# A fused RWKV-7 and GELU kernel: each piece of weights in four transfers of 2560-byte rows in place of one of 10240-byte rows

## The chip, the cores and the metric

The kernel runs on one core of a Trainium2 chip. The metric is the time of one execution on the device, in microseconds (us), given as the median of several runs. Engines are named as in the profile: PE is TensorE's matrix multiply and PEld its weight load, DVE is VectorE, ACT is ScalarE, POOL is GpSimd, and SP is SyncE, which here does nothing but issue DMA transfers. A "block" below means 256 instructions of one engine.

## The reference

Two parts follow each other. The first is a linear attention with a state per head (4 batches, 8 heads, 768 steps, head size 40), which runs through time:

```python
for t in range(S):
    y[:, :, t] = np.einsum('bhd,bhde->bhe', rt, state)
    Sa = np.einsum('bhde,bhe->bhd', state, at)
    state_decay = state * wt[:, :, None, :] - np.einsum('bhd,bhe->bhde', Sa, bt)
    state = state_decay + np.einsum('bhd,bhe->bhde', vt, kt)
```

Its output, as 3072 rows of 320, goes through a two-layer network with a hidden size of 2048:

```python
h = x @ w_in
g = h * (1.0 / (1.0 + np.exp(-1.702 * h)))
return (g @ w_out).astype(np.float32)
```

The inputs of the attention are float32. The two weight matrices, w_in (320 x 2048) and w_out (2048 x 320), come as float64 and are made into float32 on the chip.

## The kernel before

**Units and chunks.** Time is cut into 12 chunks of 64 steps. A unit is one chunk of two of the four batches, so there are 24 units, and units 2c and 2c+1 make up chunk c. For each unit the kernel forms decays, scores, a triangular inverse in five levels (`inverse`, with a transpose on DVE or a copy on ACT between levels), solves for the rows, reads the output and hands the state on to unit i+2 (`solve`). Unit i's output tile x goes out to DRAM and comes back transposed into `xT_all` (L983 and L987), because the network wants the channels on the partitions. When both units of a chunk are back, `mlp(c)` multiplies by w_in (`ps_up`), applies GELU on ACT and multiplies by w_out (`ps_down`).

**Weights.** The float64 weights come in eight pieces, four of w_in and four of w_out. A piece is 128 rows of 1280 float64 numbers: 10240 bytes a row, 1,310,720 bytes in all. `weight(n, rank, src)` loads piece n (L498) into one of four raw places: two in the tile `extra` ("a" and "b"), two in parts of `w_sb` that are not yet in use ("w4" and "w6"), and one piece in `xT_all` ("x"), so pieces 5, 6 and 7 wait until a raw place is free again. Five instructions then make float32 of a piece: one on ACT (L478, about 1.4 us), three on DVE (L482, L486, L490, about 0.8 us each where nothing holds them up), one on POOL (L494, about 3 us). The eight pieces are in flight or being converted between 13 us and 115 us of the span.

**Other loads.** Each unit loads ak, b and rv (`load`, L533, two transfers of 40 rows each, rows of 4096, 2048 and 4096 bytes), RV (128 rows of 1280 bytes), time (128 rows of 2560 bytes) and logw (L520, 1280 bytes); from unit 4 on also wc (L520, 2112 bytes).

**Order of the work.** Nothing is scheduled by hand and nothing while the kernel runs. Every piece of work is a task with a rank, the engines that can do it with a cost in ns, what it reads and writes, and a size if it is a transfer. `Plan.order` simulates the engines with these costs, and the order in which it starts the tasks is the order of the instructions on each engine. Of the tasks that are able to start, the one with the lowest rank is taken. `Plan.refined` then draws 300 random changes of ranks from a generator with a fixed seed (`TRIES, SEED`), keeps one if the simulated end comes earlier, and so changes the order of the work whose start the first simulation put before 140 us. The simulation also counts that PE's instructions come in blocks of 256 by DMA, and that this takes longer while transfers run; a transfer of over 1,000,000 bytes (`LARGE`) weighs more in this than others do:

```python
BESIDE, LARGE, BESIDE_LARGE = 0.35, 1e6, 0.63
...
took = self.FETCH + sum(w * max(0.0, min(y, at + took) - max(x, at)) for x, y, w in running[-10:])
...
wire = max(wire, end + self.LATENCY)
running.append((wire, wire + self.SPREAD * t.size / self.RATE, self.BESIDE_LARGE if t.size > self.LARGE else self.BESIDE))
```

`wire` is the simulated time at which the transfers issued so far are through; `running` holds them with their weights, and only the last ten are looked at.

**SP's queue.** SP issues all transfers, one after the other, in planned order. An issue takes 0.33 to 0.41 us in the trace (L498). The trace also shows that eight completion semaphores are taken in turn, and that an issue does not happen before the transfer that last took its semaphore, the eighth before it, has landed. The data of the transfers run on one queue, named q1 in the profile, and PE's instruction blocks come on another, q8, both over the same 16 DMA engines.

The function that the diff touches, with its calls:

Of the kernel before, what the change touches and what calls it, by code (L numbers as in the profile page):

```python
# [279 lines left out]
def rwkv7_gelu_quick(ctx: ExitStack, tc: tile.TileContext, time_d, v_d, w_d, wc_d, ak_d, b_d, rv_d, w_in, w_out, out):  # L280
    nc = tc.nc
# [5 lines left out]
    PIECE = w_in.shape[2]  # L287
# [6 lines left out]
    EARLY = 4  # L294
    BY_PE = 4
    PLAIN = 4
    ROUNDS, WINDOW, SHARE = 4, 5000.0, 1.0
    TRIES, SEED = 300, 1
    RANKS = [14, 16, 20, 24, 35, 37, 39, 41]
    HALF = [slice(0, 64), slice(64, 128)]  # L300
    BITS = (0, 1)
# [8 lines left out]
    plan = Plan(dict(logw=3, wc=3, G=1, wch=3, wz=2, time=2, ak=2, b=2, rv=2, FT=3, GT=1, kh=2, bh=2, zr=2, rz=2,  # L310
                     A=1, B=1, RV=2, E0=2, W0=2, P21=2, PT=2, W=2, E=2, ES=2, EX=2, T=2, Tc=1, QT=1, zraw=2, zT=1, M=2, x=1, xT=3, g=4, ob=1), 4)
# [17 lines left out]
    def mm(o, lhsT, rhs, start):  # L329
        nc.tensor.matmul(o, lhsT, rhs, start=start, stop=True, skip_group_check=True)  # L330
# [5 lines left out]
    def pe(*sets):  # L336

        return {"PE": sum(n * 2 * max(58.0, cols / 1.2 + 3) for n, cols in sets), "instr": sum(16 * n for n, _ in sets)}

    def dve(n):  # L340
        return {"DVE": 170.0 + 1.03 * n}

    def act(n):
        return {"ACT": 210.0 + 0.76 * n}
# [7 lines left out]
    def of(e):  # L352
        return nc.gpsimd if e == "POOL" else nc.vector
# [77 lines left out]
    def preset(engine, *places):  # L431
        for t in places:
            copy(engine)(t, one32.unsqueeze(1).to_broadcast([128, 8, 32]))
# [28 lines left out]
    def weight(n, rank, src):  # L462
        at = raws[n]
        def raw():
            if at == "x":
                return xT_all[:, 1:].rearrange("p s n -> p (s n)").bitcast(INT64)
            tile, k = spots[at]
            return tile[:, k * PIECE:(k + 2) * PIECE].bitcast(INT64)

        scale = lambda: w_sb[:, n * PIECE:(n + 1) * PIECE].bitcast(INT32)  # L470

        before = [("weight", m) for m in range(n) if raws[m] == at]
        there = [("weight", m) for m in range(n) if raws[m] in (f"w{n}", f"w{n - 1}")]
        word = lambda dt, w: raw().bitcast(dt).rearrange("p (n two) -> p n two", two=2)[:, :, w]

        def rebased(t):

            nc.scalar.activation(scale().bitcast(FP32), word(FP32, 1), ACT.Prelu, scale=2.0 ** -112, alpha=2.0 ** 32)  # L478

        def bounded(t):  # L480

            nc.vector.tensor_scalar(scale().bitcast(FP32), scale().bitcast(FP32), least, most, ALU.max, ALU.min)  # L482

        def shifted(t):

            nc.vector.tensor_single_scalar(scale(), scale(), 3, op=ALU.logical_shift_left)  # L486

        def rounded(t):

            nc.vector.tensor_single_scalar(word(INT32, 1), word(UINT32, 0), 2.0 ** -29, op=ALU.mult)  # L490

        def joined(t):

            nc.gpsimd.tensor_tensor(out=scale(), in0=scale(), in1=word(INT32, 1), op=ALU.add)  # L494

        one, add = 170.0 + 0.52 * PIECE, 200.0 + 2.1 * PIECE
        T = lambda *names: [(name, n) for name in names]
        plan.add(rank, {"SP": 350.0}, lambda t: nc.sync.dma_start(raw(), src), reads=before, writes=T("wt"), size=128 * PIECE * 8)  # L498
        plan.add(rank, act(PIECE), rebased, reads=T("wt") + there, writes=T("rebased"))
        plan.add(rank, {"DVE": one, "sbuf": True}, bounded, reads=T("rebased"), writes=T("bounded"))  # L500
        plan.add(rank, {"DVE": one, "sbuf": True}, shifted, reads=T("bounded"), writes=T("parts"))
        plan.add(rank, {"DVE": one, "sbuf": True}, rounded, reads=T("rebased"), writes=T("parts"))
        plan.add(rank, {"POOL": add}, joined, reads=T("parts"), writes=T("weight"))

    def weights():
        for n in range(len(raws)):
            weight(n, RANKS[n], w_in[n] if n < NQ else w_out[n - NQ])
# [184 lines left out]
    def inverse(i):  # L692
# [10 lines left out]
        PT = at(PT_t, i).rearrange("p (j t) -> p j t", t=96)  # L703
        if i < PLAIN:
            plan.add(R - 3, {"ACT": 400.0}, lambda t: preset(t.engine, PT[:, :, 64:]), room=T("PT"), writes=T("preset"))
        elif i < PLAIN + 2:
            plan.add(R - 3, {"ACT": 800.0, "DVE": 900.0}, lambda t: preset(t.engine, at(E0_t, i), at(W0_t, i)[:, :, 32:]), room=T("PT"),
                     writes=T("preset"))

        def score_N(t):  # L710

            ps = psum(t, "ps_N")
            for f, u in product(BITS, BITS):
                for e, b in QUARTERS:
                    o, j = (2 * f + u) * 64, slot(b, u, f)
                    mm(ps[HALF[b], e, o:o + 64], ahT()[HALF[e], j], b_of(i)[HALF[e], j], o == 0)
        plan.add(R, pe((4, 64)), score_N, reads=T("ahT", "bhT") + (T("preset") if i < PLAIN + 2 else []), uses=T("ak", "b"), room=T("E0", "P21"), pair=("N", i))
        for n in BITS if i >= PLAIN else ():
            plan.add(R, dve(256), lambda t, n=n: nc.vector.copy_predicated(  # L719
# [4 lines left out]
                 writes=T("P21"), pair=("N", i))  # L724
        if i >= PLAIN:
            plan.add(R, {"DVE": 430.0, "POOL": 750.0, "sbuf": True}, lambda t: of(t.engine).tensor_sub(  # L726
                at(W0_t, i)[:, :, :32], two32.unsqueeze(1).to_broadcast([128, 8, 32]), at(E0_t, i)), reads=T("E0"), writes=T("W0"))

        def turned(rank, source, reads, n, dst, writes):

            plan.add(rank, dve(256), lambda t: nc.vector.transpose(ES(n), source(t)), writes=[key("ES", n, 6)], **reads)  # L731

            def spread(t):
                if t.engine == "ACT":
                    for h in BITS:
                        nc.scalar.activation(dst[:, :, h], ES(n), ACT.Copy, scale=quads[:, h, :1])  # L736
                else:
                    of(t.engine).tensor_mul(dst, ES(n).unsqueeze(2).to_broadcast([128, 8, 2, 32]),
                                            quads.unsqueeze(1).to_broadcast([128, 8, 2, 32]))
            plan.add(rank, {"POOL": 1390.0, "DVE": 700.0, "ACT": 910.0, "sbuf": True}, spread, reads=[key("ES", n, 6)], writes=writes)  # L740

        if i >= PLAIN:
            turned(R, lambda t: at(E0_t, i), dict(reads=T("E0")), 0, EX(0), [key("EX", 0, 5)])
# [411 lines left out]
```

## Time and profile before

| what | value |
|---|---|
| median of 3 runs | 713.35 us (712.49 to 715.39) |
| the profiled execution, its own time | 715.64 us |
| its span, first to last instruction | 713.9 us |
| PE busy | 673.0 us, 94% of the span |
| DVE, ACT, POOL busy | 59%, 49%, 29% |
| packets of 10240 bytes (weights), from the trace's record of packets | 1024, median 388 ns each |
| packets of 2560 bytes (time) | 6144, median 102 ns, three quarters below 127 ns |
| packets of 16384 bytes on q8 (instruction blocks) | 159, median 1048 ns |

The page's rows of digits cut the span into 40 slices of 17.8 us and give in tenths how busy each engine is in each slice, what part of full speed the clock granted to PE, and how busy the DMA engines are. The windows view gives the same as numbers for stretches that one chooses. A timeline lists an engine's instructions in order; in square brackets stands the idle time before an instruction and what ended it. "issue" there means that nothing that the profile shows ended it: no semaphore came, the instruction simply wasn't there earlier. The chain of waits follows the work that ended last back from the end.

### The profile page before, as it was taken

The page shows a single profiled execution, that of the slowest core. Times are in us where ns is not written, and L with a number is a line of the kernel's source. Part 1 is how long each engine was busy: PE and PEld are TensorE (multiplying, and loading weights), DVE is VectorE, ACT ScalarE, POOL GpSimd, SP SyncE. Part 2 cuts the span into 40 slices and gives each one's busy share as a digit, 9 for nine tenths or more (in the row PEclk, how much of TensorE's full clock was granted, in tenths as well). Part 3 has the DMA queues.
Part 4 walks back from the last instruction along what each step waited for, and adds up shares of the span by engine and source line. Part 5 has one row for each costly group of instructions (what it writes and reads, how often), then busy time and mean ns, then how long its engine had stood idle before and what let it go on. Part 6 is the DMA issues. An engine that isn't in the chain of part 4 may idle for free.

```text
span 713.9 us, 43522 instructions
## 1 busy us (share of the span) xinstructions
PE 673.0 (94%) x20256; PEld 562.4 (79%) x20256; DVE 423.8 (59%) x747; ACT 347.7 (49%) x683; POOL 204.6 (29%) x260
## 2 busy tenths in 40 slices
PE   4667899999999999999999999999999999999997
PEld 4566779887888788788888998779978788877563
DVE  6689777756766576577474775666675656421000
ACT  4465636656365465454555565256445535342020
POOL 5367244442431321331342233220341320200000
PEclk9879999999999999999999999999999999999999
DMA  7955351431441341341432241251341230111000
GB/s 244 394 193 181 111 168 47 139 99 44 129 121 32 113 137 32 111 139 42 120 121 86 72 124 50 83 147 33 107 115 32 81 96 5 41 49 31 20 3 19
DMA packets 31860, 69.81 MB, mean 98 GB/s; under 512 B 5056, under 2 KB 14272, under 8 KB 30656
## 3 DMA queue, kind: packets, MB, share of 16 engines
q1 hardware_dynamic: 31680, 67.03, 30.5%
q8 instruction: 159, 2.61, 1.5%
q14 instruction: 21, 0.17, 0.1%
HBM read 59.15 MB, written 7.86 MB: 94 GB/s over the span
## 4 chain that ended last, share of the span: by engine, by line
PE 88%; DVE 5%; issue 3%; DMA 2%; ACT 1%; SPq 0%; ACTq 0%; DVEq 0%
PE ps_down L330 29%; PE ps_up L330 28%; PE ps_level L330 9%; PE ps_y L330 4%; PE ps_B L330 4%; PE ps_X L330 2%; PE ps_T L330 1%; PE ps_Q L330 1%; PE ps_rz L330 1%; PE ps_A L330 1%; PE ps_RV L330 1%; PE ps_N L330 1%; PE ps_zT L330 1%; PE ps_cum L330 1%; DMA rv<-in_rv 1%
## 5 line engine op out<-in xcount | busy, mean ns | idle before, releaser
L330 PE MATMUL ps_up<-xT_all,w_sb 64*64 64x256 f32 x3840 | 251.7, 378 | 1.8 <-issue 1.7
L330 PE MATMUL ps_down<-w_sb,g 64*64 64x320 f32 x3072 | 243.0, 431 | 0.8 <-issue 0.6
L330 PEld LDWEIGHTS ps_up<-xT_all,w_sb 64*64 64x64 f32 x3840 | 157.5, 133 | 27.1 <-issue 2.7
L330 PEld LDWEIGHTS ps_down<-w_sb,g 64*64 64x64 f32 x3072 | 131.1, 133 | 45.4 <-issue 2.4
L736 ACT ACTIVATE EX<-ES,quads 128x256 f32<-128x256 f32 x124 | 56.2, 501 | 56.8 <-DVE ES L731 56.4
L1008 ACT ACTIVATE g<-ps_up 128x1024 f32<-128x1024 f32 x48 | 49.1, 1024 | 39.6 <-PE ps_up L330 39.4
L330 PEld LDWEIGHTS ps_level<-W,EX 64*64 64x64 f32 x2560 | 57.5, 134 | 8.3 <-ACT zT L878 1.0
L780 ACT COPY W<-ps_level 128x512 f32<-128x512 f32 x55 | 32.2, 586 | 55.3 <-PE ps_level L330 54.7
L657 POOL TENSOR_TENSOR kh<-time,G 128x320 f32<-128x320 f32 x23 | 20.9, 910 | 131.9 <-PE ps_y L330 70.7
L330 PE MATMUL ps_level<-W,EX 64*64 64x64 f32 (+1 forms) x2560 | 55.7, 218 | 0.9 <-ACT zT L878 0.6
L782 DVE TENSOR_TENSOR E<-two,ps_level 128x256 f32<-128x256 f32 x80 | 33.2, 415 | 39.1 <-ACT W L780 38.7
L1034 DVE TENSOR_TENSOR ob<-ob,ps_down 128x320 f32<-128x320 f32 x24 | 11.6, 482 | 59.6 <-ACT ob L1032 58.7
L726 POOL TENSOR_TENSOR PT<-two,PT 128x256 f32<-128x256 f32 x18 | 13.1, 728 | 109.8 <-DVE PT L719 105.1
L330 PE MATMUL ps_level<-PT,EX 64*64 64x64 f32 (+2 forms) x1280 | 37.5, 250 | 5.0 <-issue 4.0
L330 PEld LDWEIGHTS ps_level<-PT,EX 64*64 64x64 f32 x1280 | 35.4, 152 | 7.9 <-issue 4.9
L973 POOL TENSOR_TENSOR x<-zr,FT 128x128 f32<-128x128 f32 x80 | 40.9, 539 | 0.0
L731 DVE STREAM_TRANSPOSE ES<-E 128x256 f32<-128x256 f32 x80 | 35.6, 444 | 3.9
L911 ACT COPY B<-ps_B 128x416 f32<-128x416 f32 x38 | 19.1, 504 | 37.2 <-PE ps_B L330 36.9
L330 PE MATMUL ps_y<-RV,kh 64*64 64x104 f32 x768 | 35.7, 251 | 1.4 <-DVE M L927 1.4
L330 PE MATMUL ps_y<-M,bh 64*64 64x104 f32 x768 | 35.6, 249 | 1.2 <-issue 1.2
L649 POOL TENSOR_TENSOR ak<-ak,FT 128x512 f32<-128x512 f32 x16 | 21.5, 1345 | 50.0 <-DMA ak<-in_ak 31.0
L1032 ACT COPY ob<-ps_down 128x320 f32<-128x320 f32 x22 | 9.4, 425 | 53.1 <-PE ps_down L330 53.0
(136 smaller groups left out, 1168.1 us busy)
## 6 DMA issues: line engine op xcount, KB each, us to landing
time<-in_time SPq DMA_DIRECT2D x24, 320.0 KB
ak<-in_ak SPq DMA_DIRECT2D x48, 160.0 KB
rv<-in_rv SPq DMA_DIRECT2D x48, 160.0 KB
xT_all<-x_dram SPq DMA_DIRECT2D x48, 160.0 KB
wc<-in_wc SPq DMA_DIRECT2D x20, 264.0 KB
logw<-in_w SPq DMA_DIRECT2D x24, 160.0 KB
RV<-in_v SPq DMA_DIRECT2D x24, 160.0 KB
b<-in_b SPq DMA_DIRECT2D x48, 80.0 KB
```

What stands on the lines that cost most here:

```text
L330: nc.tensor.matmul(o, lhsT, rhs, start=start, stop=True, skip_group_check=True)
L649: plan.add(R, {"DVE": 690.0, "POOL": 1270.0, "sbuf": True}, lambda t: of(t.engine).tensor_mul(ahT(), ahT(), FT_of(i)), reads=T("ak", "FT") ...
L657: plan.add(R + 4, {"POOL": 870.0, "DVE": 490.0, "sbuf": True}, lambda t, n=n, dst=dst: of(t.engine).tensor_mul(dst(i)[:, :, :D], by_head(t ...
L726: plan.add(R, {"DVE": 430.0, "POOL": 750.0, "sbuf": True}, lambda t: of(t.engine).tensor_sub(at(W0_t, i)[:, :, :32], two32.unsqueeze(1).to ...
L731: plan.add(rank, dve(256), lambda t: nc.vector.transpose(ES(n), source(t)), writes=[key("ES", n, 6)], **reads)
L736: nc.scalar.activation(dst[:, :, h], ES(n), ACT.Copy, scale=quads[:, h, :1])
L780: plan.add(rank, any2(512), lambda t: copy(t.engine)(tiles_of(W(n + 1)), blocks(psum(t, ""), 64)), writes=[key("W", n + 1, 5)], pair=pair)
L782: plan.add(rank, dve(256), lambda t: nc.vector.tensor_sub(tiles_of(E(n + 1)), every(two32, [128, 2, 4, 32]), blocks(psum(t, ""), 64)[:, :, ...
L911: plan.add(R, any2(416), lambda t: copy(t.engine)(dst(), psum(t, "")[:, :, :208]), writes=[("Bv", i)] if x and c > 0 else T("B"), pair=(na ...
L973: of(t.engine).tensor_mul(x[:, b ^ u, b], both(i)[:, at, :64], FT_of(i)[:, at])
L1008: plan.add(-45, {"ACT": 1030.0, "table": "gelu"}, lambda t: nc.scalar.activation(g_of(c * NQ + q).rearrange("p m r n -> p r m n"), psum(t, ...
L1034: plan.add(-45, dve(320), lambda t: nc.vector.tensor_add(ob_of(serial), ob_of(serial), psum(t, "")[:, 1, :DM]), reads=[("ob", serial)], wr ...
```

## The change

The plan's task that loads a piece with one transfer becomes four tasks of the same rank, each with its own transfer of a quarter of every row: 128 rows of 2560 bytes, 327,680 bytes. They write the same raw place, and the first conversion step (L478) reads what all four wrote, so it still starts when the whole piece has landed. Each of the four tasks is planned with 350 ns of SP and a quarter of the size, and none of them is over `LARGE` any more. The seed of the plan's random search goes from 1 to 2.

```diff
+    PARTS = 4
     ROUNDS, WINDOW, SHARE = 4, 5000.0, 1.0
-    TRIES, SEED = 300, 1
+    TRIES, SEED = 300, 2
...
-        plan.add(rank, {"SP": 350.0}, lambda t: nc.sync.dma_start(raw(), src), reads=before, writes=T("wt"), size=128 * PIECE * 8)
+        for g in range(PARTS):
+            some = slice(g * PIECE // PARTS, (g + 1) * PIECE // PARTS)
+            plan.add(rank, {"SP": 350.0}, lambda t, some=some: nc.sync.dma_start(raw()[:, some], src[:, some]),
+                     reads=before, writes=T("wt"), size=128 * PIECE * 8 // PARTS)
         plan.add(rank, act(PIECE), rebased, reads=T("wt") + there, writes=T("rebased"))
```

## The prediction

> **What bounds the kernel now.** I read the page's busy digits first, then the windows view, then the chain of waits and the waits of PE and SP, and last PE's timeline at the places these named.
>
> ```profile
> PE   4667899999999999999999999999999999999997
> ...
> PEclk9879999999999999999999999999999999999999
> DMA  7955351431441341341432241251341230111000
> GB/s 244 394 193 181 111 168 47 139 99 44 129 121 32 113 137 32 111 139 42 120 121 86 72 124 50 83 147 33 107 115 32 81 96 5 41 49 31 20 3 19
> ```
>
> From the sixth slice on (89 us) PE is nearly always busy; from 150 us to the end it works 553.6 of 564 us (windows view). What a change in the transfers can win lies before that. Up to 102 us PE has 29.8 us of gaps over 0.25 us, DMA runs at up to 394 GB/s, and the clock granted to PE drops. PE's waits from 0 to 150 us:
>
> ```profile
> PE ps_level L330 <- issue: 5.5, 3, 2.4
> PE ps_N L330 <- DMA ak<-in_ak: 5.2, 1, 5.2
> PE ps_cum L330 <- ACT logw L556: 3.8, 1, 3.8
> PE ps_X L330 <- DVE T L853: 3.3, 2, 2.9
> PE ps_cumc L330 <- issue: 2.1, 1, 2.1
> ...
> PE ps_up L330 <- issue: 1.7, 1, 1.7
> PE ps_RV L330 <- issue: 1.3, 1, 1.3
> ```
>
> Columns: total us, times, longest. The "issue" waits are 10.7 us, and no semaphore ends them. Numbering PE's instructions in the trace (matmuls and weight loads together), they come before numbers 706, 963, 1219, 3011, 3267 and 4802: distances of 257, 256, 7 x 256, 256 and 6 x 256 - 1. So they stand at block boundaries, and what is missing is the next 256 instructions. The chain of waits shows that the end hangs on them (start, length, what):
>
> ```profile
> 21.58 1.55 issue
> ...
> 27.70 2.10 issue
> ...
> 34.70 1.56 issue
> ...
> 72.35 2.43 issue
> ```
>
> The record of packets has, for each block, the 16384-byte packet on q8. I count its delay from the moment the block before begins to execute. The five blocks that begin at 16.87, 23.13, 29.80, 68.26 and 94.88 us, with a piece of weights on the wire, have delays of 3.97, 4.32, 3.76, 3.97 and 4.27 us, mean 4.06; their packets take 1.0 to 1.15 us, and the next block begins 1.2 to 1.6 us after that. Those are the five stalls of 1.55, 2.10, 1.56, 2.43 and 1.74 us (the last at 99.71). The sixth, 1.33 us at 66.93, has a delay of only 1.24 and no weights near it. The windows view over these blocks:
>
> ```profile
> 16.87:23.13 6.26, 3.48 (x137) 2.93 (x130) 4.90 (x6) 3.54 (x6) 3.99 (x4) 1.00 1.01 417
> 23.13:29.80 6.67, 4.57 (x128) 4.33 (x128) 4.80 (x7) 1.60 (x2) 0.00 (x0) 0.74 1.01 414
> ...
> 59.70:64.25 4.55, 3.30 (x135) 2.85 (x128) 4.55 (x5) 2.14 (x4) 3.70 (x3) 1.00 0.75 232
> 68.26:74.78 6.52, 3.23 (x128) 2.50 (x128) 4.94 (x9) 3.89 (x7) 1.92 (x3) 0.98 0.86 307
> ```
>
> Columns: length, then busy us of PE, PEld, DVE, ACT, POOL, then clock, DMA share, GB/s. Under weights a block lasts 6.3 to 6.7 us whatever PE's work in it (3.2 to 4.6).
>
> **The change part by part.**
>
> *Rows a quarter as long: the instruction blocks.* Each of the 16 DMA engines gets 8 rows of a 128-row transfer: 8 x 388 ns = 3.10 us at 10240 bytes, 8 x 102 = 0.82 us at 2560. With idle wires the delay is 0.72 to 1.01 us (blocks from 79.66, 87.06, 91.30), so 4.06 is idle plus one transfer's rows on the engine. Blocks that began under time loads, rows of 2560 bytes, had 2.07 (from 59.70), 1.99 (74.78) and 1.95 us (189.31). I take 2.0: 2.06 us less. The stalls of 1.55, 1.56 and 1.74 go; of 2.10 and 2.43 some 0.04 and 0.37 stay. Removed: 1.55 + 2.06 + 1.56 + 2.06 + 1.74 = 8.97 us. What is late next is the engines that these blocks wait for, DVE above all. Bounds: a delay of 4.06 still (nothing gained; four transfers may pass an engine as one did), or 0.72 (all 9.4 us).
>
> *How much of that reaches the end.* The stall at 99.71 lies where PE is the bound: 1.74 us in full. The first three (5.17 us) lie in the chain of units 0 and 1, and DVE waits with them: it idles 1.47, 2.57, 0.81 and 1.08 us between 22.3 and 38.3 us and is then busy nearly through to 73. If DVE's stretch starts earlier it meets its data: ak of unit 2 lands at 42.15 us, and POOL takes it up at 45.5, so 3.4 us can be gained before that transfer is late (b: landed 40.4, used 47.2; time: 37.3, 52.1). I take 3.4. The stall at 72.35 I take at nothing: PE reaches the first `ps_up` at 79.23, and the last xT for it lands at 79.26, so a PE that is early waits for xT; bound 2.06. Sum: 3.4 + 1.74 = 5.1 us.
>
> *The clock.* It is 0.5 from 23.3 to 26.7, 30.2 to 33.6, 37.0 to 43.8, 47.2 to 50.6 and 74.5 to 77.9 us, mostly behind stretches in which PE stood. With fewer stalls some of these stay at full clock: blocks 23.13 and 29.80 (4.57 and 4.72 us of PE at 0.74) would take 1.2 us less each. Not counted in the forecast; 2.4 us for the low end.
>
> *The transfers themselves.* 4 x 102 = 408 ns against 388, so 8 x 20 = 0.16 us a piece, 0.8 for the five that run behind each other from 17 to 36 us; by the 127 ns of the upper quarter 0.96 a piece. Five of eight conversions start later than their piece lands (second piece: landed 24.66, ACT at 35.0; fifth: 36.34, 45.6), which hides it; ACT waits for the last two pieces (1.7 us in two waits), and without cover it costs 0.2 us each, at most 1. I take 0.
>
> *SP and its eight semaphores.* 24 more issues of 0.33 to 0.41 us, about 0.45 with what lies between: 1.35 us a piece. Behind them in SP's queue stand the loads of unit 2, and later x and xT. Already now:
>
> ```profile
> SPq L533 <- DMA extra<-in_w_in: 5.7, 2, 3.0
> ```
>
> The b load of unit 2 is issued at 20.67 because a piece landed at 20.61. Issues lag more with four semaphores a piece, but eight quarter pieces are 2.6 MB, 6.2 us of wire at 420 GB/s, and an issue needs about 2.5 us to its landing (time: 57.93 to 60.45), so the wire doesn't run dry and the landings stay. Cost 0. At 65.65 to 68.56 us, between piece 6 and x, SP has room for the 1.35 us; without it x is 1.35 us later.
>
> [...] Here two whole pieces land 3.10 us apart (24.66, 27.76), 423 GB/s with no fixed part to be seen. [...]
>
> *Another order.* Quarters are under the planner's limit for large transfers, and the seed is new, so the static order of the opening changes in places that no row shows. One long wait of the kind that order makes is 2.9 us (`ps_X` for DVE's T, 43.82 to 46.70). I take 0, with 2.9 either way.
>
> The sum against the profiled execution: 715.64 - 5.1 = 710.5, a ratio of 0.9928; the same share of the median 713.35 gives **708.2 us**.
>
> **The rivals.**
>
> - *The opening swallows it.* DVE is busy from 39 to 73 us, and xT's landing sets the first `ps_up`; if the time won before 36 us is given back there, only the stall at 99.71 remains: 713.35 - 1.74 = 711.6. For it: DVE's 9 to 10 us of every 10 from 60 to 70. Against: DVE's stretch begins with idle time that ends on PE.
> - *Everything counts.* All 8.97 us and 2.4 us of clock: 702.0. For it: four of the five are on the chain. Against: the landing of ak and xT.
> - *It doesn't shorten the fetch.* If an engine lets all queued rows of q1 pass before q8, delays stay at 4 us: 713.4. Against: 2.0 us under time loads; for: those were single transfers, never four in a row.
> - *Slower: x behind more weights.* x of unit 1 is issued at 68.56, behind piece 6 (65.65), and its trip back ends at 79.26, where PE's full stretch begins. If the new order frees a raw place sooner, so that piece 7 goes ahead of x as well, xT is later by 8 x 4 x 127 ns = 4.06 and four issues, 1.8, and piece 6 adds 0.96: 6.8 us, less 1.74: 718.4. It decides once xT lands over 5.3 us later than now (5.3 - 1.74 = 0.5%). Against: today piece 7 leaves at 94.15, 25 us after x.
>
> **How the numbers follow.** 0.5% is about what a measurement of this kernel can tell from no change: 3.6 us, so 709.8 to 716.9 is "same". Chances: forecast 0.43 (705.3 to 711.1 with the 2.9 of order), swallowed 0.22, everything 0.15, fetch not shortened 0.08, slower 0.12. Under 709.8: three quarters of the forecast, everything, and some of swallowed with a lucky order: 0.53. Over 716.9: 0.13. The rest is 0.34. The range leaves out half of "everything" and most of "slower": 702 to 716.
>
> **What would show it.** Right: the blocks under weights begin 4.2 to 4.7 us apart instead of 6.5, q8's delay there is near 2 us, PE's issue waits up to 150 us sum to 1.5 to 3 us, the first `ps_up` starts at 75 to 77 us, and the half-speed stretches get fewer. Wrong: delays near 4 us; or short delays with the first `ps_up` still at 79 (swallowed); or xT landing after 80 us (slower). The later 600 us should keep their length; if they differ, it is the order, which I can't price.

## The result and the profile after

The changed kernel takes 713.84 us (median of 12 runs, 709.44 to 718.05), the kernel before 713.55 us in the runs beside it (12 runs, 708.92 to 716.7). The ratio is 0.9995, 95% interval 0.9973 to 1.0018: no difference that can be measured. The forecast was 708.2 us.

The profiled execution of the changed kernel has a span of 713.0 us. Its busy digits from the page, to be laid beside those of before:

```profile
PE   4677899999999999999998999999999999999997
...
PEclk9869999999999999999999999999999999999999
DMA  7984552334231441341432241251341230111000
GB/s 244 326 269 120 176 165 83 96 86 121 73 112 42 116 125 32 111 140 41 126 115 86 71 124 51 79 153 33 111 114 33 78 95 5 41 50 30 20 3 19
```

The weights are spread out more (the second slice moves 326 GB/s instead of 394, the third 269 instead of 193), and PE's opening has the same shape. PE's waits from 0 to 150 us:

```profile
PE ps_level L331 <- DVE EX L756: 7.7, 5, 3.3
...
PE ps_level L331 <- issue: 2.9, 4, 1.8
PE ps_y L331 <- issue: 2.2, 1, 2.2
PE ps_X L331 <- issue: 2.0, 1, 2.0
...
PE ps_A L331 <- issue: 1.4, 1, 1.4
```

The waits that no semaphore ends are 8.8 us in all, against 10.7 before; 1.5 to 3 were forecast for success. (1.4 of the 8.8 us end at 126.87, where no weights are loaded any more.) What was a wait of 0.9 us for DVE's transposes is now 7.7. All gaps of PE over 0.25 us up to 150 us make 30.2 us, against 29.8. The first `ps_up` starts at 80.14 us, not earlier than before (79.23). The windows view over four of PE's blocks of 256 instructions, with the columns as in the prediction:

```profile
16.11:22.15 6.04, 3.68 (x138) 2.96 (x130) 4.17 (x6) 3.88 (x10) 4.40 (x4) 0.95 1.00 343
22.15:26.75 4.60, 4.23 (x127) 3.99 (x126) 2.79 (x4) 1.12 (x2) 0.00 (x0) 0.70 0.88 298
...
37.95:44.16 6.21, 4.19 (x140) 3.90 (x136) 3.41 (x7) 3.27 (x7) 1.91 (x1) 0.67 1.00 311
44.16:51.40 7.24, 4.77 (x129) 4.37 (x129) 2.81 (x4) 2.62 (x5) 1.03 (x1) 0.76 0.92 272
```

Of the six blocks from 16.11 to 51.40, all beside weights, four still last 6 to 7 us, though PE works 3.7 to 4.8 us of that; the two from 22.15 and 26.75 last 4.60 and 4.83. From the record of packets, the delays of their successors (from the beginning of a block to the packet on q8) are 2.68, 2.34, 2.54, 3.68, 3.69 and 4.70 us in these six blocks, and 2.91 from 95.45: 3.2 in the mean. Three of them came within 0.7 us of the 2.0 that the forecast took, none reached it; the longest is longer than any before. The block from 44.16 ends in a stall of 2.20 us in the middle of `ps_y`, and DVE waits 3.8 us behind it for ACT's copy of y.

### The profile page after: what moved, and what is told of

Its sections match the earlier page's. It is cut to its first block, busy times and chain, and to the rows that moved or that the text cites. A ratio compares the mean times of both kernels' runs of the same rounds, so it can differ in the third digit from the quotient of the medians.

```text
span 713.0 us, 43601 instructions
## 1 busy us (share of the span) xinstructions
PE 672.9 (94%) x20256; PEld 566.1 (79%) x20256; DVE 425.2 (60%) x743; ACT 345.1 (48%) x676; POOL 214.5 (30%) x267
## 4 chain that ended last, share of the span: by engine, by line
PE 87%; DMA 6%; DVE 3%; issue 1%; SPq 1%; ACT 1%; DVEq 0%; ACTq 0%
PE ps_down L331 29%; PE ps_up L331 29%; PE ps_level L331 7%; PE ps_y L331 4%; PE ps_B L331 4%; PE ps_X L331 2%; PE ps_A L331 2%; PE ps_Q L331 1%; PE ps_T L331 1%; PE ps_N L331 1%; PE ps_rz L331 1%; DMA ak<-in_ak 1%; PE ps_RV L331 1%; PE ps_zT L331 1%; DMA w_sb<-in_w_in 1%
## 5 line engine op out<-in xcount | busy, mean ns | idle before, releaser
L331 PEld LDWEIGHTS ps_up<-xT_all,w_sb 64*64 64x64 f32 x3840 | 159.8, 133 | 24.5 <-issue 1.4
L1038 DVE TENSOR_TENSOR ob<-ob,ps_down 128x320 f32<-128x320 f32 x24 | 11.5, 480 | 59.6 <-ACT ob L1036 59.5
L331 PE MATMUL ps_level<-PT,EX 64*64 64x64 f32 (+2 forms) x1280 | 35.5, 245 | 11.1 <-DVE EX L756 7.7
L331 PEld LDWEIGHTS ps_level<-PT,EX 64*64 64x64 f32 x1280 | 32.8, 146 | 15.4 <-DVE EX L756 5.5
L653 POOL TENSOR_TENSOR ak<-ak,FT 128x512 f32<-128x512 f32 x18 | 24.7, 1373 | 48.0 <-DMA ak<-in_ak 24.9
L931 DVE TENSOR_TENSOR M<-ps_X,later 128x832 f32<-128x832 f32 x24 | 24.4, 1018 | 19.2 <-PE ps_X L331 19.2
```

Of the source, the lines that this page charges most:

```text
L653: plan.add(R, {"DVE": 690.0, "POOL": 1270.0, "sbuf": True}, lambda t: of(t.engine).tensor_mul(ahT(), ahT(), FT_of(i)), reads=T("ak", "FT") ...
L931: plan.add(R + 1, dve(832), lambda t: nc.vector.tensor_tensor(M_of(i).rearrange("p (j b) n -> p b j n", b=2), psum(t, "")[:, :, :416].rear ...
```

## The experiments

The theories after the result: A, quarter rows win as forecast, and the new order gives it back; B, a wire kept full by quarters holds the instruction blocks back as long as one kept full by whole rows; C, the blocks come sooner, but DVE and the way of x to xT swallow it. The delays told of below were read from the record of packets in the same way as in the prediction. That record does not name a packet's engine, so "to an engine" means a sixteenth of all. A ratio is to the kernel before, run on the same chip.

### e1 and e10: quarter rows in the old order

Nothing is planned differently; the one planned task issues four transfers.

```diff
+        def loaded(t):
+            for g in range(4):
+                some = slice(g * PIECE // 4, (g + 1) * PIECE // 4)
+                nc.sync.dma_start(raw()[:, some], src[:, some])
-        plan.add(rank, {"SP": 350.0}, lambda t: nc.sync.dma_start(raw(), src), reads=before, writes=T("wt"), size=128 * PIECE * 8)
+        plan.add(rank, {"SP": 350.0}, loaded, reads=before, writes=T("wt"), size=128 * PIECE * 8)
```

> The plan of before, order untouched on every engine; each weight task issues four transfers of 2560-byte rows. In the changed kernel PE's issue waits stayed at 8.9 us against 10.7. Theory A (the transfers win, the new order gives it back): delays of the instruction blocks under weights near 2.5 us instead of 4.06, issue waits under 5 us, ratio to before 0.99 to 0.995. Theory B (a queue kept full by quarters holds the blocks back nearly as long): delays of 3 to 4 us, ratio 0.998 to 1.002. Theory C (shorter blocks, but DVE and xT swallow it): delays near 2.5 us, first ps_up still at 78 to 79.5 us, ratio 0.996 to 0.999.

Measured: 715.07 us, ratio 1.0013 (0.9978 to 1.0047). The delays under the first pieces were 3.83, 2.04, 2.84 and 3.49 us, the issue waits up to 150 us 11.6 us. Ratio and waits are those of B; the delay of 2.04 is that of A, and 2.84 lies between the two. So I took a second profile:

> A second profile of the order of before with quarter rows. In its first profile the blocks that began at 12.0, 18.5, 23.5 and 28.5 us had delays of 3.83, 2.04, 2.84 and 3.49; the kernel with only five pieces in quarters had 1.22, 4.09, 4.22 and 3.80 at the same place. If quarters shorten the delay on average, it is 2 to 3.5 in the three blocks under the first pieces again; if chance decides, as likely 3.8 to 4.3.

There the blocks from 16.38, 22.74, 29.50 and 68.28 have delays of 4.00, 4.42, 3.85 and 3.63 us, and the windows view shows blocks as long as those of the kernel before:

```profile
16.38:22.74 6.36, 3.71 (x138) 2.96 (x131) 4.28 (x6) 4.12 (x11) 4.53 (x4) 1.00 1.03 379
22.74:29.50 6.76, 4.57 (x127) 4.32 (x126) 4.83 (x7) 1.60 (x2) 0.00 (x0) 0.75 1.04 395
...
68.28:74.24 5.96, 4.26 (x128) 3.56 (x128) 5.15 (x9) 2.51 (x4) 2.14 (x4) 0.70 0.90 276
```

In the second of them 601 packets of 2560 bytes pass on q1 before the one on q8, some 37 to an engine; in the same block of before it was 170 of 10240 bytes, some 11 to an engine (and some 120 of 2112 bytes in both). A is out: with the old order there is nothing to give back.

### e2, e3 and e8: the new order, the new seed and the split, each alone

e2 takes the whole order of the changed kernel, but the first of the four tasks issues the whole piece:

```diff
-            plan.add(rank, {"SP": 350.0}, lambda t, some=some: nc.sync.dma_start(raw()[:, some], src[:, some]),
+            plan.add(rank, {"SP": 350.0}, lambda t, g=g: nc.sync.dma_start(raw(), src) if g == 0 else None,
```

> The plan and the order of the changed kernel on every engine, but the first of a piece's four tasks issues the whole piece with 10240-byte rows and the other three issue nothing. Theory A: slower than before by as much as quarters win in the order of before, ratio 1.005 to 1.01, and delays back at 4 us. Theory B: the ratio of the changed kernel, 0.998 to 1.002. Theory C: 1.000 to 1.004.

e3 is before with another seed, e8 the changed kernel with the old one:

```diff
-    TRIES, SEED = 300, 1
+    TRIES, SEED = 300, 2
```

> Before with the second seed alone: one transfer and one task a piece. Theory A leaves open whether seed or task split costs; if the seed, ratio 1.005 to 1.01, if not, 0.998 to 1.002. Theories B and C: 0.997 to 1.003, the scatter of one order against another.

> The changed kernel with the old seed: four planned tasks a piece, seed 1. Together with before, the second seed alone and the changed kernel it tells the seed from the split into tasks. If the orders that the planner draws differ by no more than the runs scatter, ratio 0.996 to 1.003 and the gaps of PE up to 105 us between 26 and 31 us, as in the other four; if the split makes worse orders with seed 1, 1.005 or more.

Measured: e2 717.01 us, ratio 0.9987 (0.9952 to 1.0022), with delays of 3.4 to 3.7 us in its three blocks of pure weights; e3 713.35 us, 0.9969 (0.9942 to 0.9997); e8 716.01 us, 1.0047 (1.002 to 1.0074). The gaps of PE up to 150 us are 31.0, 27.5 and 30.7 us. So whole rows in the new order are no slower than before, and one order against another is worth some 0.3 to 0.5% either way: with one transfer the new seed was 0.3% faster, with four the old seed 0.5% slower and the new one even. This is as much as the change was hoped to bring.

### e4: the same four transfers, cut the other way

```diff
-                some = slice(g * PIECE // 4, (g + 1) * PIECE // 4)
-                nc.sync.dma_start(raw()[:, some], src[:, some])
+                some = slice(32 * g, 32 * g + 32)
+                nc.sync.dma_start(raw()[some], src[some])
```

> The order of before, four transfers a piece, but each is 32 whole rows of 10240 bytes: two rows on each of the 16 DMA engines. It tells the number of transfers from the length of rows. If a block waits for the rows of one transfer, it waits 2 x 388 = 0.78 us instead of 3.1: delays of 1.5 to 2 us and a ratio at or under that of the quarter rows. If it waits for the bytes or descriptors that are queued, whatever transfer they belong to: delays near 4 us, ratio 0.998 to 1.002.

Measured: 737.02 us, ratio 1.0279 (1.0239 to 1.0319), which neither side expected. The windows view over its blocks shows why it tells nothing of the question:

```profile
16.10:25.00 8.90, 3.77 (x130) 3.02 (x129) 4.28 (x6) 2.62 (x10) 4.44 (x4) 0.82 1.02 204
25.00:34.20 9.20, 4.60 (x127) 4.36 (x126) 5.70 (x8) 2.98 (x3) 0.00 (x0) 0.69 1.02 215
```

The DMA engines are as full as before (last column but one), but move 204 and 215 GB/s; before moved 415 and 396 in the same windows. A packet of 10240 bytes has a median of 775 ns instead of 388. The delays are 6.15, 6.62 and 6.92 us, against 3.97, 4.32 and 3.76 in before: beside the slower wire the blocks were held back for longer.

### e5: nearly no weights on the wire

Each transfer brings a sixteenth of a row, and five fills on POOL give the rest a value:

```diff
-        plan.add(rank, {"SP": 350.0}, lambda t: nc.sync.dma_start(raw(), src), reads=before, writes=T("wt"), size=128 * PIECE * 8)
+        plan.add(rank, {"SP": 350.0}, lambda t: nc.sync.dma_start(raw()[:, :PIECE // 16], src[:, :PIECE // 16]), reads=before, writes=T("wt"), size=128 * PIECE * 8)
...
+    rest = slice(PIECE // 8, 2 * PIECE)
+    nc.gpsimd.memset(extra[:, rest], 0.0)
```

> The order of before, but each weight transfer brings only the first 640 bytes of a row, a sixteenth; the rest of the raw places is filled with zeros by POOL in its idle time, so the weights that are used are wrong and the work on all engines is that of before but for five fills. It takes nearly all weight bytes off the wire, more than any way of cutting a piece can. Swallowed: the stalls at 21.6, 27.7, 34.7, 72.4 and 99.7 us are gone and the first ps_up comes at 72 to 76 us, but by the third x (96.4 us in before) not more than 2 us of it is left, ratio 0.994 to 0.999. The wire decides: the whole 9 us of stalls stay won, third x at 86 to 89 us, ratio 0.985 to 0.99.

Measured: 706.82 us, ratio 0.9931 (0.9909 to 0.9953). Three of the blocks beside which the weights ran:

```profile
17.67:22.67 5.00, 4.43 (x124) 4.30 (x127) 1.94 (x4) 3.24 (x6) 4.33 (x4) 0.66 0.75 240
22.67:27.20 4.53, 3.25 (x140) 2.80 (x129) 4.42 (x6) 2.07 (x3) 4.53 (x4) 1.00 0.82 266
27.20:32.80 5.60, 3.00 (x127) 2.52 (x131) 5.55 (x6) 3.33 (x12) 3.19 (x3) 1.00 0.30 102
```

Their delays are 1.55, 1.22 and 1.12 us; the third is long for another reason, PE waits for DVE. An earlier block, from 11.74, still has a delay of 3.34 us and a stall of 1.80 behind it: there 60 KB of other loads for the most part went ahead to an engine. So it need not be weights. The first `ps_up` starts at 73.76 us, 5.5 before that of before, and the third x leaves at 91.48, 4.9 before 96.41. So neither expectation held: the lead stays, which refutes C, but taking all weight bytes off the wire is worth 0.7%, 4.9 us, and not the 9 us of stalls. The waits for what comes after them grew: 4.6 us for DVE's transposes, 4.0 for DVE's T, 3.0 for POOL's T, where the first profile of before has 0.9, 3.3 and 1.9.

### e6: the kernel before once more

> The kernel of before, a second profile, for the scatter from one execution to the next: the five stalls under weights and the first ps_up at 79.2 us within 0.5 us, if the opening repeats itself, and other stalls after 150 us (4.2 us of gaps in the first profile), if the scatter of several us between runs comes from there.

The first `ps_up` came at 77.51 us, 1.7 earlier than in the first profile, with the same instructions in the same order. Its issue waits up to 150 us:

```profile
PE ps_level L330 <- issue: 5.7, 5, 2.2
...
PE ps_cumc L330 <- issue: 2.1, 1, 2.1
...
PE ps_RV L330 <- issue: 1.3, 1, 1.3
PE ps_up L330 <- issue: 1.0, 2, 0.8
```

The stalls beside weights are 2.21, 2.15, 0.72 and 1.12 us at the first four places and none over 0.25 at the fifth: 6.2 us, where the first profile had 9.4. The delays there are 3.95, 4.48, 3.07, 2.24 and 2.60, 3.3 in the mean, with whole rows: about as low as in the changed kernel. The opening does not repeat itself to 0.5 us. Against this profile e5's lead is 3.8 us at the first `ps_up` and 4.0 at the third x. The gaps after 150 us are 4.3 us, 4.2 in the first profile, though in e1 they were 7.6.

### e7: five pieces in quarters, three whole

```diff
+            parts = 4 if n < 5 else 1
```

> The order of before, only the first five pieces (on the wire from 13 to 36 us) in quarter rows, the last three whole. Swallowed: the first ps_up comes 1 to 2.5 us before that of before, the third x (96.4 us) within 0.5 us of it, and the stall of 1.7 us near 99 us is there. Otherwise the lead of 1 to 2.5 us is still there at the third x.

One run: 712.26 us. The first `ps_up` starts at 77.52 us, the third x leaves at 95.05: as in e6 (77.51 and 95.44), which has no quarters at all. Under the quarters the delays are 4.09, 4.22 and 3.80 us, with 646, 573 and 489 packets of 2560 bytes ahead. There is no lead that could be swallowed.

### e9: the disputed cost by itself

A kernel with nothing but PE blocks and weight loads:

```python
block(12)                                   # PE; SP waits for the end of these
for n in range(20): whole(n, bufs[n % 8])   # up to eight in flight
block(20)
for n in range(20): quarters(n, bufs[n % 8])
block(20)
for n in range(16): whole(n, bufs[0])       # each waits for the one before
block(20)
for n in range(24): quarters(n, bufs[0], 0)
block(20)
```

> The disputed cost by itself; nothing of the reference is computed and the output is zeros. PE runs blocks of 128 weight loads and 128 small matmuls (64x64 by 32 columns) without end, so that a block lasts about as long as the next one takes to arrive. Beside them SP loads weights in five stages: nothing; 20 whole pieces of 10240-byte rows, up to eight in flight; 20 pieces in quarters of 2560-byte rows, up to eight quarters in flight; 16 whole pieces, one in flight; 24 quarters, one in flight. Rows of one transfer decide (the working of the prediction): delays of 1, 4, 2, 4 and 2 us in the five stages. Bytes in flight decide: 1, 4, 4, 4 or less, and 2 or less. Rows decide, whatever is in flight, is told from bytes by the third stage alone.

The windows view over the five stages (none, whole, quarters, whole one at a time, quarters one at a time):

```profile
5.00:40.00 35.00, 34.15 (x1255) 33.62 (x1252) 0.00 (x0) 0.00 (x0) 0.00 (x0) 1.00 0.02 4
50.00:110.00 60.00, 36.05 (x1280) 34.73 (x1278) 0.00 (x0) 0.00 (x0) 0.00 (x0) 1.00 0.99 417
146.00:206.00 60.00, 38.04 (x1343) 36.58 (x1340) 0.00 (x0) 0.00 (x0) 0.00 (x0) 1.00 1.03 399
245.00:335.00 90.00, 57.30 (x2037) 55.59 (x2040) 0.00 (x0) 0.00 (x0) 0.00 (x0) 1.00 0.58 207
350.00:410.00 60.00, 58.74 (x2124) 57.55 (x2120) 0.00 (x0) 0.00 (x0) 0.00 (x0) 1.00 0.36 97
```

PE's work is the same in each; the count of matmuls tells how fast the blocks come. In 60 us PE gets 1280 matmuls beside whole rows and 1343 beside quarters, 5% more, against 2124 beside single quarters. The delays: 1.03 to 1.59 us with an idle wire, from the fourth block on (0.39 to 0.76 in the first three); 3.51 to 4.00 beside whole rows (ten blocks, mean 3.72); 2.93 to 3.71 beside quarters (ten blocks, mean 3.48); mostly 2.9 to 5.2 beside whole pieces one at a time; 1.05 to 1.44 beside single quarters. The third stage decides for B: quarters shorten the delay by 0.24 us, not by 2.06. The fourth shows that it isn't the number of transfers in flight either. The fifth tells less than it seems, since a quarter took as long as a block (about 3.5 us) and few packets fell into the delay.

Of the theories put down ahead of e9, bytes in flight fits all five stages (1, 4, 4, 4 or less, 2 or less). A count of bytes agrees with it: what SP had issued and no packet had yet carried when a block began, and what then went ahead of the block's packet on q8, both to an engine. In twelve blocks of the fourth stage a whole piece stood there, 80 to 82 KB, and 80 to 82 KB went ahead. In the ten blocks beside quarters it is 75 to 115 KB and 78 to 98, in the ten beside whole rows 232 to 597 KB and 97 to 118. In the fifth stage at most 19 KB stood there. So nearly all that was queued went ahead of the block, up to some 118 KB, in rows of either length.

### e11 and e12: a version that leaves gaps on the wire

If gaps free the blocks, the four pieces that aren't urgent can go one quarter at a time:

```diff
+        parts = 4 if n >= 4 else 1
+        for g in range(parts):
+            some = slice(g * PIECE // parts - (g > 0), (g + 1) * PIECE // parts)
+            plan.add(rank, {"SP": 350.0}, lambda t, some=some: nc.sync.dma_start(raw()[:, some], src[:, some]),
+                     reads=before + (T(f"landed{g - 1}") if g else []), writes=T("wt", f"landed{g}"), size=128 * PIECE * 8 // parts)
```

> Seed 1; pieces 0 to 3 (w_in) whole as in before, pieces 4 to 7 (w_out) in quarters that overlap by one column, each planned after the landing of the one before, so that SP issues it only then and the wire has gaps. If gaps and not short rows free the instruction blocks, the blocks beside the quarters have delays of 1.1 to 2 us and the stalls of 2.43 and 1.74 us (72 and 99 us in before) are under 0.5 us; the two stalls beside the whole pieces stay at 1.5 to 2.2 us. Worth at most 4 us, ratio 0.994 to 1.000, with the scatter of a new order on top (the other four orders: 0.997 to 1.005). If quarters one after the other still hold blocks back, delays of 3 us or more remain beside them.

> The same with seed 2, for a second draw of the order. Same delays as the kernel before it; ratio 0.992 to 1.000, as seed 2 alone had 0.997. If the two seeds differ by over 0.5% here, the order is worth more than the blocks.

Measured: e11 713.89 us, ratio 1.0017 (0.9991 to 1.0042); e12 715.47 us, 1.0045 (1.0016 to 1.0075). Beside the single quarters the delays are 0.4 to 2.0 us, at or under the 1.1 to 2 expected, and no stall of over 0.7 us that nothing ends lies between 50 and 150 us in e11 (its two beside whole pieces, 1.52 and 2.31 us, are there). It isn't faster: PE's gaps up to 150 us are 27.3 and 30.0 us, because the new orders wait elsewhere (e11: 3.0 us for ACT's conversion of a piece in front of PE's level, 2.8 and 1.5 us for DVE's transposes). No version that computes the reference's result beats both kernels by more than an order's scatter.

## Why the prediction was wrong, point by point

- **What bounds the kernel, and what the stalls are**: right. The issue waits stand at block boundaries in every profile (e9 too; the numbers in the prediction count PE's semaphore instructions along with matmuls and weight loads), and they follow the traffic: delays of 1.1 to 1.6 us in e5's three blocks, 3.5 to 4 in e9 under a stream of whole pieces.
- **"I take 2.0: 2.06 us less"**: this is the step that failed. The 2.0 was read beside time loads, which are single transfers of 2560-byte rows with nothing of their kind behind them (35 and 15 KB to an engine went ahead in the blocks from 59.70 and 74.78), and then used for a stream of such transfers. In a stream the delay is 3.48 us by itself (e9) and 3.6 to 4.4 in the kernel (e7, e10); e1 had 2.0 to 3.8 and the changed kernel 2.3 to 4.7, in the mean 3.1 and 3.2, where the kernel before has 4.06 in its first profile and 3.3 in e6. The model "idle plus one transfer's rows on the engine" fitted the whole rows by coincidence: eight rows are 3.10 us, but in e9's stream 9.5 to 11.5 went ahead, and eight only where no more were queued. The bound that the prediction named, "four transfers may pass an engine as one did", is what happens: 37 quarter rows pass on an engine where 11 whole rows did (e10). The rival that the fetch isn't shortened, which said this of "all queued rows of q1", had 0.08.
- **How much of it reaches the end**: 8.97 us of stalls came from one profile. A second one of the same kernel has 6.2 us (e6), and with nearly all weight bytes gone the kernel wins 4.9 us (e5, 0.9909 to 0.9953). My 5.1 us was thus about the price of having no weight traffic at all. That something behind the stalls would cut the gain was right: e5 kept 4.9 of 9. What cut it there was not what the prediction named. PE's waits for DVE and POOL grew, there is no wait for ak behind the first stalls (its loads that went out at 27.82 us go out at 19.09), and the weight loads of the first `ps_up` wait 0.5 us for xT. In the first profile of before, PE began `ps_up` at 79.23, ahead of the landing at 79.26 that the prediction has it wait for; in e1 it does wait for xT, 1.1 us. The rival "swallowed" was wrong: e5's lead of 5.5 us at the first `ps_up` is still 4.9 at the third x (3.8 and 4.0 against e6).
- **The clock**: the half-speed stretches up to 150 us add up to 20.5 us in the first profiles of before and after, and to 13.7 in e5 and in e6 alike. They differ as much from run to run as from kernel to kernel.
- **Rows of a quarter** (408 ns for four against 388): right, 399 GB/s against 417 in e9 is 4%, and ACT's waits for a piece stayed at 1.6 us, 1.7 before. **SP and its semaphores**: cost 0 holds for e1 and e10 in sum.
- **Another order**, taken at 0 with 2.9 us either way: its size was right. The orders tried here differ by 0.3 to 0.5% (e3, e8, e12). The changed kernel has 1.9 us less of issue waits and more waits for DVE; whether its order or its fetches give the even sum can't be told apart at this scatter.
- **The slower rival** (x behind more weights) didn't happen: xT lands at 79.6 us, 79.26 before.

What stays open: what holds the rows that pass. In e9's streams 31 to 38 quarter rows, 78 to 98 KB, or 9.5 to 11.5 whole ones, 97 to 118 KB, pass on each engine; that fits a limit in bytes or time better than one in rows. No stage had an amount in flight between one quarter (20 KB) and one piece (82 KB), and in the kernel it isn't as regular: e1's delay of 2.04 us has 77 KB queued and only 53 ahead.

## What to carry to other kernels

Take the price of a transfer's neighbour from a row with the same state of the queue, not only the same size of rows: beside lone transfers of 2560-byte rows the delays were 1.95 to 2.07 us (before), beside a stream of them 2.93 to 3.71 (e9). What counted here was the bytes queued at that moment, up to some 118 KB to an engine, and up to eight quarters in flight still queued 75 to 115. Before cutting a transfer into pieces, measure what is won when it isn't there at all (here 0.7%); that bounds every way of cutting it. Where a planner's order changes with the edit, make one run with the old order kept and one with the new order alone, since here an order was worth as much as the edit was hoped to be.

## What the runs showed of the hardware that was not expected

- A load of 32 partitions ran at half speed (e4): 204 and 215 GB/s with the engines full, where before moved 415 and 396 in the same windows, and 775 ns a packet of 10240 bytes against 388.
- The runs of the kernel before on one chip lie 5 to 11 us apart (709.62 to 714.83 on one, 17 runs; 709.5 to 720.37 on another, 29 runs). Stalls at block boundaries come and go between executions: those of before beside weights summed to 9.4 and 6.2 us in two profiles, and e1 had a stall of 2.0 us at 387.6 us of the span, where before's first profile has none, one reason why its profiled span was 717.3 us in spite of a first `ps_up` at 77.34.
- The chain of waits of the changed kernel puts much of 18 to 52 us on weight transfers. At 52.55 us it says that ACT's copy of y (L969) waited for the last quarter of a piece, but in the built order ACT waits for PE alone there, at the copy right before it (L960), which ran from 52.23 to 52.66: ACT was not idle. The two events only coincide. A chain that jumps to a transfer should be checked against what the instruction waits for.
